# The first pair's queries in two column halves, its keys in one transfer, and an order that allows for late landings

## The chip, the cores and the metric

The kernel runs on one core of a Trainium2 chip. The metric is the device time of one execution in microseconds (us), the median of several runs. One more execution was recorded by the hardware profiler. Its span runs from the first instruction to the last, and all times of day below are counted from the start of that span.

The engines are PE (TensorE, matrix products and transposes), DVE (VectorE), ACT (ScalarE), POOL (GpSimd) and SP (SyncE, which here only issues transfers). Each engine works through its own list of instructions strictly in order: an instruction that waits holds everything behind it on that engine.

## What is computed

Attention with 4 batches and 8 heads of 768 tokens and 64 channels, in which a query sees only the keys of its own hash bucket, and behind it a gated layer over all 3072 tokens:

```
q_bits = (q @ proj > 0);  k_bits = (k @ proj > 0)          # 6 bits for each token
mask   = bucket(q_bits)[:, None] == bucket(k_bits)[None, :]
scores = where(mask, q @ k.T / sqrt(64), -1e9)
attn   = exp(scores - max);  attn = attn / (sum(attn) + 1e-9)
x      = attn @ v                                           # gathered to (3072, 512)
out    = (sigmoid(x @ w_gate) * (x @ w_val)) @ w_out        # 512 -> 1536 -> 512
```

## The kernel before

The kernel works on pairs of heads. There are 16 pairs, and each has six steps of 128 queries, in two groups of three (NG = 2, GT = 3). Pair 0 differs from the others: nothing runs ahead of it, so its preparation stands open at the start of the program.

The names that matter are these. `kr` and `wide` (later `qr`) are the keys and queries as loaded, `vr` the values. `tk`, `tq` and `ts` are their transposes on PE; `ts` is the query block with the two heads swapped. `kx`, `qx` and `sx` are copies of the transposes in SBUF. Each is split into a high part (`kh`, `qh`, `qsh`) and a low remainder (`kl`, `ql`, `qsl`), so that three products give nearly full precision. `hw` holds the projection, and `w0` (row name `w`) a padded copy of it, made on DVE by `hash_weights`. `hk` and `hq` are the hash products of pair 0, and `kb` and `qb` the bits that come out of them. One score task (`sc`) is a product of bits plus three products of high and low parts. `e` is the masked minimum of the scores, then their exponential; `tp` is its transpose, `ef` the copy of that, `pv` the product with the values, `rd` and `rb` the way of the row sums through memory, and `xs` the result, stored to `xd`.

The gated layer's weights come as 64-bit numbers. `converted` loads one (`raw...`) and rebuilds it as 32-bit numbers in four DVE passes, one ACT pass and one POOL pass; `split` makes its high and low parts, and for most of them writes these out to a kept copy in memory (`kg`, `kv`, `ko`), from where `fetch_piece` brings them back when the gated layer proper begins. Ten such pieces form one slot; the first slot's names are `wg_4`, `wv_4` and `wo_4`. The products of the early part of the gated layer (`zg`, `zv`, `zo`) are mixed with the attention of the next batch; the steps `z1g`, `z2g` and so on and `yo` follow after it.

A planner sets the order of everything. Each task has a key (its priority, in steps of attention), an engine or several to choose from, a duration, and the tasks that it follows. `Plan.order` plays this through in time, and the tasks are written out in the order in which it starts them. For a transfer it assumes a time to landing. For PE it also knows three forms of tiles (rows for `sc` and the transposes, columns for `pv` and the later hashes, all for the 128x128 products), and it stays in one form for as long as `PATIENCE` allows. Thirty products without a use (`busy`, row name `idle`, 128x512) fill PE where the plan has nothing else for it. Keys `W_KEY` and `W_STEP` set when a weight may be loaded and how far apart the weights lie.

## Time and profile before

| what | value |
|---|---|
| median of 3 runs | 999.85 us (997.95 to 1000.48) |
| the profiled execution's own time | 997.94 us |
| its span | 996.2 us |
| PE busy | 969.6 us, 97% of the span |
| DVE busy | 775.6 us (78%) |
| ACT busy | 554.0 us (56%) |
| POOL busy | 271.9 us (27%) |
| moved by DMA | 190.95 MB, mean 192 GB/s |

The profiled execution lies 1.74 us above its span and at the lower end of the timed runs. A busy PE need not be useful: the fillers count as busy, and so does a product that runs at half clock.

### The profile page before, as it was taken

To read this page: it belongs to the slowest core of one execution; us is meant where nothing else is said; L and a number is where in the kernel's file an instruction comes from. 1 tells how busy PE (TensorE), PEld (TensorE's weight loads), DVE (VectorE), ACT (ScalarE), POOL (GpSimd) and SP (SyncE) were. 2 spreads that over 40 slices of the span, in tenths; PEclk is the share of its full clock that TensorE was granted. 3 is DMA by queue.
4 is the path that set the end of the run, shared out by engine and by line. 5 is a ranking of instruction groups with operands and counts; after the bars stand their busy time and mean duration, and the time that the engine had idled before them with its cause. 6 is when DMAs were issued, how large, how long until landed. Compare 5 with 4: busy or idle time off the path is not lost.

```text
span 996.2 us, 20856 instructions
## 1 busy us (share of the span) xinstructions
PE 969.6 (97%) x8092; PEld 777.3 (78%) x8092; DVE 775.6 (78%) x1460; ACT 554.0 (56%) x1015; POOL 271.9 (27%) x245
## 2 busy tenths in 40 slices
PE   7999999999999999899999999999999999999998
PEld 4555567676666666666689989989989999999897
DVE  6778888897889778687567879887687778787864
ACT  4868788787877778787643434333323325242330
POOL 2252566546666556552012131100000000000000
PEclk9999999999999999999999999999999999999999
DMA  6456576667776766656368969477479570514121
GB/s 134 125 135 169 162 203 202 209 200 217 233 211 222 236 194 204 190 169 236 107 233 292 356 234 354 171 234 276 141 233 337 198 275 16 175 44 147 43 85 63
DMA packets 144250, 190.95 MB, mean 192 GB/s; under 512 B 64632, under 2 KB 102936, under 8 KB 144152
## 3 DMA queue, kind: packets, MB, share of 16 engines
q1 hardware_dynamic: 142520, 189.24, 59.2%
q8 instruction: 63, 1.03, 0.4%
q10 hardware_dynamic: 1568, 0.39, 0.2%
q14 instruction: 35, 0.29, 0.1%
q0 software_dynamic: 64, 0.00, 0.0%
HBM read 127.41 MB, written 49.28 MB: 177 GB/s over the span
## 4 chain that ended last, share of the span: by engine, by line
PE 83%; DVE 7%; DMA 4%; ACT 3%; SPq 2%; issue 1%; POOL 1%; DVEq 0%; ACTq 0%; POOLq 0%
PE yo L876 17%; PE pv L1235 10%; PE sc L1167 7%; PE tp L1218 6%; PE zv L535 3%; PE zo L568 3%; PE sc L1161 3%; PE zg L535 3%; DVE e L1177 3%; PE z1g L757 2%; PE z7g L757 2%; PE z4v L757 2%; PE z1v L757 2%; PE z5g L757 2%; PE z4g L757 2%; PE z3g L757 2%
## 5 line engine op out<-in xcount | busy, mean ns | idle before, releaser
L1185 ACT ACTIVATE e<-e,st 128x768 f32<-128x768 f32 x192 | 178.7, 932 | 50.0 <-DVE e L1177 49.6
L1177 DVE TENSOR_SCALAR_CACHE_REDUCE e<-sc 128x768 f32<-128x768 f32 x192 | 176.0, 952 | 23.4 <-PE sc L1167 22.4
L1235 PE MATMUL pv<-ef,vr 128*64 128x384 f32 x768 | 139.5, 495 | 0.0
L1218 PEld LDWEIGHTS tp<-ident,e 64*128 64x128 f32 x2304 | 83.8, 138 | 42.2 <-issue 16.6
L1225 DVE COPY ef<-tp 128x768 f32<-128x768 f32 x93 | 87.7, 951 | 20.2 <-PE tp L1218 20.0
L1218 PE MATMUL tp<-ident,e 64*128 64x64 f32 x2304 | 96.3, 226 | 7.0 <-DVE e L1177 3.4
L1225 ACT COPY ef<-tp 128x768 f32<-128x768 f32 x99 | 77.7, 794 | 27.3 <-PE tp L1218 26.9
L1235 PEld LDWEIGHTS pv<-ef,vr 128*64 128x64 f32 x768 | 48.8, 136 | 53.8 <-issue 47.3
L1167 PE MATMUL sc<-kh,ql 64*128 64x384 f32 x192 | 90.2, 470 | 0.0
L1167 PE MATMUL sc<-kh,qsl 64*128 64x384 f32 x192 | 90.1, 469 | 0.0
L1161 PE MATMUL sc<-kb,qb 64*128 64x384 bf16 x384 | 65.0, 331 | 9.5 <-DVE e L1177 5.8
L1167 PE MATMUL sc<-kh,qh 64*128 64x384 f32 x192 | 64.2, 335 | 0.0
L1167 PE MATMUL sc<-kh,qsh 64*128 64x384 f32 x192 | 64.2, 334 | 0.0
L1167 PE MATMUL sc<-kl,qsh 64*128 64x384 f32 x192 | 64.0, 334 | 0.0
L1167 PE MATMUL sc<-kl,qh 64*128 64x384 f32 x192 | 64.0, 333 | 0.0
L1161 PEld LDWEIGHTS <-qb 64*128 64x128 bf16 x384 | 22.2, 94 | 49.3 <-issue 41.1
L777 ACT COPY snm1g<-z1g 128x384 f32<-128x384 f32 x20 | 9.6, 478 | 84.4 <-PE z1g L757 84.3
L1245 POOL TENSOR_TENSOR xs<-xs,rb 128x384 f32<-128x384 f32 x32 | 33.4, 1044 | 69.1 <-DVE xs L1242 41.9
L876 PE MATMUL yo<-wo,gh 128*128 128x512 f32 x144 | 44.5, 390 | 0.0
L1056 POOL TENSOR_TENSOR kl<-kx,kh 128x768 fp32r<-128x768 f32 x16 | 29.3, 1833 | 42.1 <-ACT kh L1053 26.1
L915 DVE TENSOR_TENSOR ol<-yo,ol 128x512 f32<-128x512 f32 x36 | 24.8, 688 | 19.6 <-PE yo L876 19.4
L535 PE MATMUL zg<-xh,wg 128*128 128x384 f32 x128 | 37.5, 348 | 0.1
(591 smaller groups left out, 2812.7 us busy)
## 6 DMA issues: line engine op xcount, KB each, us to landing
wg<-kg SPq DMA_DIRECT2D x33, 512.0 KB
wv<-kv SPq DMA_DIRECT2D x33, 512.0 KB
ra<-xd SPq DMA_DIRECT2D x32, 384.0 KB
wo<-ko SPq DMA_DIRECT2D x22, 512.0 KB
part<-ob SPq DMA_DIRECT2D x36, 256.0 KB
kg<-pkg SPq DMA_DIRECT2D x15, 512.0 KB
kv<-pkv SPq DMA_DIRECT2D x15, 512.0 KB
kr<-in_k_dram SPq DMA_DIRECT2D x64, 96.0 KB
```

What stands on the lines that cost most here:

```text
L535: nc.tensor.matmul(z["acc"][:, :GN], a[:, wc], x[xx][c // 2][:, c % 2, :], start=(c == 0 and i == 0), stop=(c == KC - 1 and i == 2),)
L568: nc.tensor.matmul(acc, a[:, slot, ts_], w, start=(first and i == 0), stop=(last and i == 2))
L757: nc.tensor.matmul(bank[m], a[:, wc], x[xx, block][:, c, :], start=(c == 0 and i == 0), stop=(c == 1 and i == 2),)
L876: nc.tensor.matmul(accs[t], a[:, ts_], w, start=(start and jj == 0 and q == 0), stop=(stop and jj == 1 and q == 2),)
L1161: nc.tensor.matmul(sc[:, j, :GN], z["qb"][rows, beyond if j else c], z["kb"][rows, h], start=True, stop=False, tile_position=(j * D, 0),)
L1167: nc.tensor.matmul(sc[:, j, :GN], q_[rows, c], z["k" + x][rows, h * GN : (h + 1) * GN], start=False, stop=(m == 2), tile_position=(j * D, 0),)
L1177: nc.vector.tensor_scalar(sp(e), gz["sc", t, h][:, :, :GN], MASKED, None, op0=ALU.min, op1=ALU.min, accum_out=gz["st", t][:, h : h + 1],)
L1185: nc.scalar.activation(e, e, AF.Exp, bias=st[:, h : h + 1], scale=-1.0, accum_out=gz["su"][:, h * GT + t : h * GT + t + 1],)
L1218: nc.tensor.transpose(tp[:, r, at_ : at_ + D], gz["e", t, h][rows, c * P : (c + 1) * P], ident[rows, rows], tile_position=(r * D, 0),)
L1225: copy(gz["ef", c].rearrange("p (n r d) -> p r n d", r=2, d=D), gz["tp", c][:, :, :GN].rearrange("p r (n d) -> p r n d", d=D),)
L1235: nc.tensor.matmul(gz["pv"][rows, :GN], z["v"][:, h, c], gz["ef", c][:, h * GN : (h + 1) * GN], start=(c == 0), stop=(c == NC - 1), tile_p ...
L1245: nc.gpsimd.tensor_mul(gz["xs"], gz["xs"], gz["rb"])
```

## The change

Six things change.

1. Keys: each pair's keys come in one transfer (128x2x384) instead of four (128x3x64 each), and `pv` reads the values in the matching order.
2. Projection: its two small transfers are issued by SP, right behind the first keys, instead of by POOL behind its memsets. DVE clears `hw` first of all.
3. Pair 0's queries: `qx`, `qh`, `ql`, `sx`, `qsh`, `qsl`, the query hash and its bits are made in two column halves (`first_pair`). The first group's scores need only the first halves.
4. Planner: transfers may carry a slack (500 to 1500 ns) that is added to the assumed landing before anything that follows is placed.
5. `PATIENCE` goes from 9000 to 12000 for rows and from 1000 to 1500 for columns.
6. Weights: the first load is allowed at key 6 instead of 8, the first six lie 3 apart instead of 2.2, the rest start at key 26 and lie by 2.3.

The core of the diff:

```diff
-PATIENCE = dict(rows=9000, columns=1000, all=1500)
+PATIENCE = dict(rows=12000, columns=1500, all=1500)
...
-                    landed = 0
+                    landed, more = 0, ()
                     if t.dmas:
-                        n_, moved = t.dmas
+                        n_, moved, *more = t.dmas
...
-                    seen = free[e] + (landed or SEEN[e])
+                    seen = free[e] + (landed + sum(more) if landed else SEEN[e])
...
-            nc.gpsimd.dma_start(hw["w"][half * D : (half + 1) * D, at_ : at_ + NB], proj)
+            nc.sync.dma_start(hw["w"][half * D : (half + 1) * D, at_ : at_ + NB], proj)
...
-    W_KEY, W_STEP = 8.0, 2.2
+    W_KEY, W_STEP = 6, 2.3
...
-    def dma(key, nbytes, emit, **kw):
-        return add(key, "sp", 550, emit, dmas=(1, nbytes / 355), **kw)
+    def dma(key, nbytes, emit, slack=0, **kw):
+        return add(key, "sp", 550, emit, dmas=(1, nbytes / 355, slack), **kw)
...
-        a = dma(key, 600000, load, after=after + last_load[late], take=[raw_])
+        a = dma(key, 600000, load, slack=1500, after=after + last_load[late], take=[raw_])
...
-                z[n] = stage1.tile([P, 2, GT, 2, D], F32, name=f"kr{u}", tag="kr", bufs=stock["kr"])
-                from_ = k[b, two].rearrange("h (p c) d -> p h c d", c=NC)
-                for h in range(2):
-                    for j in range(2):
-                        eng.dma_start(z[n][:, h, :, j], from_[:, h, j * GT : (j + 1) * GT])
+                z[n] = stage1.tile([P, 2, NC, D], F32, name=f"kr{u}", tag="kr", bufs=stock["kr"])
+                eng.dma_start(z[n], k[b, two].rearrange("h (p c) d -> p h c d", c=NC))
...
+        def plain_swapped(j, part):
+            if j == 0 and part == 0:
                 z["sx"] = xp.tile([P, S], F32, name="sx", tag="xr1")
-            rows, first = halves[j], (1 - j) * D
-            to = ordered(z["sx"])[rows]
-            from_ = z["t", "s"][rows, :, first : first + GN].rearrange("p r (m d) -> p r m d", d=D)
+            rows, first = halves[j], (1 - j) * D + part * GT * D
+            from_ = z["t", "s"][rows, :, first : first + GT * D].rearrange("p r (m d) -> p r m d", d=D)
+            nc.scalar.activation(ordered(z["sx"])[rows, :, thirds[part]], from_, AF.Copy, scale=-SCALE)
...
+        def plain_half(part, eng):
+            if part == 0:
+                z["qx"] = stage1.tile([P, S], F32, name=f"qx{u}", tag="qx", bufs=1)
+            to, from_ = ordered(z["qx"])[:, :, thirds[part]], turned_("q")[:, :, thirds[part]]
...
+        def high_half(x, part, copy):
+            if part == 0:
+                for a_ in "hl":
+                    z[x + a_] = at.tile([P, S], F32R, name=f"{x}{a_}{u}", tag=f"{x}{a_}")
+            copy(z[x + "h"][:, parts_[part]], z[{"q": "qx", "qs": "sx"}[x]][:, parts_[part]])
...
+        def low_half(x, part, eng):
+            c = parts_[part]
+            eng.tensor_sub(z[x + "l"][:, c], z[{"q": "qx", "qs": "sx"}[x]][:, c], f(z[x + "h"][:, c]))
...
+        def hash_first(n, which):
+            if which[0] == 0:
+                z["hs", n] = ps2.tile([P, 2, 512], F32, name=f"h{n}{u}", tag="two")
+            hs = z["hs", n]
+            for m in which:
...
+        def first_pair(needs):
+            both = dict(take=["port"], give=["port"])
+            swap = add(t0 - 2.95, "pe", 2 * NC * TH, turn_swapped, after=[here["q"], last_turn], take=["two"], kind="turn")
+            kh_ = add(t0 - 3.9, "act", 735, lambda: high("k", nc.scalar.copy), after=plains)
+            kl_ = add(t0 - 3.9, "pool", 1850, lambda: low("k", nc.gpsimd), after=[kh_])
+            hk = add(t0 - 3, "pe", 4 * MM * 2, lambda: hash_first("k", (0, 1)), after=plains + [hw["task"]], take=["two"])
+            kb_ = add(t0 - 3.5, "dve", 560, lambda: bits_first("k", 0), after=[hk])
+            kb2 = add(t0 - 3.49, "dve", 560, lambda: bits_first("k", 1), after=[hk], give=["two"])
+            needs[0].extend([kl_, kb_, kb2])
+            last, hq = None, None
+            for p_ in range(2):
+                n_ = t0 - 2.9 + 2.4 * p_
+                qx = add(n_, [("dve", 480, lambda p_=p_: plain_half(p_, nc.vector)), ("act", 430, lambda p_=p_: plain_half(p_, nc.scalar))][:1 + p_],
+                         after=[last_turn, last], take=["qx"] * (p_ == 0), give=["two"] * p_)
+                last = qx
+                hq = add(n_, "pe", 4 * MM, lambda p_=p_: hash_first("q", (p_,)), after=[qx, hw["task"], hq], take=["two"] * (p_ == 0))
+                qb_ = add(n_ + 0.1, "dve", 560, lambda p_=p_: bits_first("q", p_), after=[hq], give=["two"] * p_)
+                qh = add(n_, [("dve", 300, lambda p_=p_: high_half("q", p_, nc.vector.tensor_copy)), ("act", 430, lambda p_=p_: high_half("q", p_, nc.scalar.copy))][:1 + p_],
+                         after=[qx])
+                ql = add(n_, "dve", 480, lambda p_=p_: low_half("q", p_, nc.vector), after=[qh], **both)
+                sx = add(n_, "act", 430, lambda p_=p_: plain_swapped(0, p_), after=[swap])
+                swap = sx = add(n_, "act", 430, lambda p_=p_: plain_swapped(1, p_), after=[sx], give=["two"] * p_)
+                sh = add(n_, [("act", 430, lambda p_=p_: high_half("qs", p_, nc.scalar.copy)), ("dve", 300, lambda p_=p_: high_half("qs", p_, nc.vector.tensor_copy))],
+                         after=[sx])
+                sl = add(n_ + 0.1, [("dve", 480, lambda p_=p_: low_half("qs", p_, nc.vector)), ("pool", 950, lambda p_=p_: low_half("qs", p_, nc.gpsimd))][:1 + p_], after=[sh], **both)
+                needs[p_].extend([qb_, ql, sl])
+            heads_done.extend(needs[0] + needs[1])
...
+            n: add(t0 - 10.72, "act" if i == 0 and n == "q" else "sp", 1300 if n == "q" else 600,
+                   lambda n=n: load(n, nc.scalar if i == 0 and n == "q" else nc.sync), dmas=(2, 1860, 500 * (i > 0)) if n == "q" else (1, 1360, 500 * (i > 0)), take=[n + "r"],
+                   after=(first_loads[:3] if i == 1 else first_loads if i == 2 else []) + [last_loads.get(n)])
...
-            first_loads.extend(here.values())
-            hw["loaded"] = add(t0 - 10.5, "pool", 1200, load_projection)
-            hw["landed"] = add(0, "timer", 0, lambda: None, after=[hw["loaded"], add(0, "timer", 4000, lambda: None)])
...
+            hw["loaded"] = add(t0 - 10.5, "sp", 1100, load_projection, after=[here["k"]] * 0, dmas=(2, 60))
+            hw["task"] = add(t0 - 10, "dve", 1300, hash_weights, after=[hw["loaded"]])
+            first_loads.extend(list(here.values()) + [hw["loaded"]])
...
+            attend(i, g, z, needs if i else needs[0] + needs[1] * g, v_here)
...
-        key += W_STEP
+        key += 3
+    key = 26
```

Since the planner sees other numbers, the order changes nearly everywhere. Three places show it. First, the head of SP's list, before:

```order
L967 DMA kr_0_241<-in_k_dram 128x3x64 x4
L980 DMA vr_0_262<-in_v_dram 128x2x384
L967 DMA kr_1_277<-in_k_dram 128x3x64 x4
L976 DMA qr_1_325<-in_q_dram 128x6x64 x2
L980 DMA vr_1_335<-in_v_dram 128x2x384
```

and now:

```order
L964 DMA kr_0_239<-in_k_dram 128x2x384
L283 DMA hw<-in_proj_dram 64x6 x2
L977 DMA vr_0_257<-in_v_dram 128x2x384
L964 DMA kr_1_272<-in_k_dram 128x2x384
L973 DMA qr_1_304<-in_q_dram 128x6x64 x2
```

The four transfers of the first keys became one, and the projection's two stand right behind it, ahead of the first values.

Second, DVE's list in the preparation of pair 0, from the last copy of the projection (`w`) to the last low part that the first scores need, before:

```order
L294 COPY w_220<-hw 64x2x12
L1045 TENSOR_SCALAR qx_0_312<-tq_0_282 128x2x6x64
L1053 CAST qh_0_320<-qx_0_312 128x768
L1025 TENSOR_SCALAR kb_172<-hk_0_317,dk_206 128x384
L1025 TENSOR_SCALAR kb_172<-hk_0_317,dk_207 128x384
L1056 TENSOR_TENSOR ql_0_321<-qx_0_312,qh_0_320 128x768
L1022 TENSOR_SCALAR qb_170<-hq_0_329,dq 128x768
L1008 TENSOR_TENSOR qsl_0_338<-sx,qsh_0_337 128x768
```

and now:

```order
L294 COPY w_220<-hw 64x2x12
L1000 TENSOR_SCALAR qx_0_307<-tq_0_274 128x2x3x64
L1008 CAST qh_0_315<-qx_0_307 128x384
L1000 TENSOR_SCALAR qx_0_307<-tq_0_274 128x2x3x64
L1012 TENSOR_TENSOR ql_0_316<-qx_0_307,qh_0_315 128x384 x2
L1030 TENSOR_SCALAR kb_172<-hk_0_312,dk_206 128x384
L1030 TENSOR_SCALAR kb_172<-hk_0_312,dk_207 128x384
L1028 TENSOR_SCALAR qb_170<-hq_0_324,dq 128x384
L1012 TENSOR_TENSOR qsl_0_331<-sx,qsh_0_330 128x384
L1028 TENSOR_SCALAR qb_170<-hq_0_324,dq 128x384
```

Each pass over 768 query columns became two over 384. The second half of `qsl` is gone from DVE (it stands on POOL now), and the bits of the second half stand behind everything that the first group's scores need.

Third, SP's list around the last kept weight of the attention stage (`ko_109`), up to the first fetch of a kept piece (`wg_4`), before:

```order
L1199 DMA rd_94<-sv_2_0_7772 4x32x32
L419 DMA ko_109<-pko_109_7713 128x1024
L1062 DMA qsh_3_7786<-qh_3_7776 64x768 x2
L1206 DMA rb_2_0_7794<-rd_94 64x384 x2
L1062 DMA qsl_3_7837<-ql_3_7777 64x768 x2
L1079 DMA qb_171<-qb_171 24x384 x2
L1086 DMA kb_173<-qb_171 12x384 x4
L980 DMA vr_3_7934<-in_v_dram 128x2x384
L1248 DMA xd_65<-xs_1_1_7903 128x384
L726 DMA wg_4_00_7966<-kg_0_116 128x1024
```

and now:

```order
L1224 DMA rd_97<-sv_3_1_8360 4x32x32
L419 DMA ko_109<-pko_109_8354 128x1024
L1231 DMA rb_3_1_8414<-rd_97 64x384 x2
L1273 DMA xd_65<-xs_3_0_8421 128x384
L726 DMA wg_4_00_8451<-kg_0_116 128x1024
```

The last kept weight stood right behind the store of row sums of the last batch's third pair (`sv_2_0`); now it stands behind that of the last group of all (`sv_3_1`), and the fetches follow after that.

On PE the list now opens with 9 fillers instead of 11, and between `hq` and the first score stand 7 instead of 13.

## Rows read from the trace of the kernel before

**Rows 1.** Windows of core 0: three stages; stretch, its length, busy time by engine, clock, DMA.

```profile
18.20:150.00 131.80, 122.51 (x1551) 79.10 (x1550) 108.33 (x223) 103.81 (x193) 54.98 (x43) 1.00 0.56 152
150.00:490.00 340.00, 332.19 (x3804) 228.55 (x3802) 275.64 (x542) 264.26 (x480) 180.83 (x160) 0.99 0.67 206
490.00:992.20 502.20, 501.85 (x2680) 463.34 (x2674) 380.46 (x655) 180.49 (x337) 30.42 (x28) 1.00 0.56 193
```

**Rows 2.** Timeline, 0 to 18.3: start, length, engine, line, operation [idle before].

```profile
0.75 2.35 SPq L967 DMA_DIRECT2D kr<-in_k_dram  x4
...
3.26 1.20 POOL L283 DMA_DIRECT2D hw<-in_proj_dram  x2
...
6.79 0.40 PE L1033 MATMUL tk<-ident,kr 64*128 64x64 f32 x6 [0.85 <-DMA kr<-in_k_dram]
...
6.99 0.57 PE L1033 MATMUL tq<-ident,wide 64*128 64x64 f32 x12
7.22 0.81 ACT L1049 ACTIVATE kx<-tk 128x768 f32<-128x768 f32 x1 [4.99 <-PE tk L1033]
...
8.65 0.17 DVE L288 TENSOR_SCALAR hw<-hw 64x6 f32<-64x6 f32 x1 [0.41 <-DMA hw<-in_proj_dram]
...
8.98 1.80 POOL L1056 TENSOR_TENSOR kl<-kx,kh 128x768 fp32r<-128x768 f32 x1 [4.52 <-ACT kh L1053]
...
9.13 1.69 DVE L293 COPY w<-hw 64x24 f32<-64x24 f32 x1
...
10.94 0.96 DVE L1045 TENSOR_SCALAR qx<-tq 128x768 f32<-128x768 f32 x1
...
10.97 2.19 PE L1014 MATMUL hk<-kx,w 128*128 128x384 f32 x4 [2.97 <-DVE w L294]
...
13.20 1.14 DVE L1025 TENSOR_SCALAR kb<-hk,dk 128x384 bf16<-128x384 f32 x2 [0.71 <-PE hk L1014]
...
14.26 0.95 DVE L1056 TENSOR_TENSOR ql<-qx,qh 128x768 fp32r<-128x768 f32 x1
...
15.31 2.97 PE L308 MATMUL idle<-sig 128*128 128x512 bf16 x13
...
15.52 1.02 DVE L1022 TENSOR_SCALAR qb<-hq,dq 128x768 bf16<-128x768 f32 x1 [0.31 <-PE hq L1014]
...
18.21 0.34 PE L1161 MATMUL sc<-kb,qb 64*128 64x384 bf16 x2
```

**Rows 3.** Windows with a low granted clock, columns as in Rows 1.

```profile
11.70:15.00 3.30, 3.30 (x7) 1.79 (x6) 2.56 (x5) 0.00 (x0) 0.00 (x0) 0.50 1.25 224
...
412.00:414.00 2.00, 2.00 (x10) 1.56 (x8) 1.41 (x4) 1.55 (x3) 1.49 (x2) 0.50 0.86 301
```

**Rows 4.** Timeline around 407: DVE, then PE.

```profile
407.29 0.43 DVE L364 TENSOR_SCALAR exv<-rawv 128x512 int32<-128x512 int32 x1 [5.36 <-DMA rawv<-in_moe_w_val_dram]
...
409.45 0.34 PE L1161 MATMUL sc<-kb,qb 64*128 64x384 bf16 x2 [2.80 <-DVE e L1177]
```

**Rows 5.** Waits, whole span: engine, line, waited for; us, times, longest.

```profile
DVE exv L364 <- DMA rawv<-in_moe_w_val_dram: 8.5, 5, 5.4
```

**Rows 6.** The chain that ended last, 363 to 376: one and two tasks of `pv`.

```profile
367.23 1.44 PE pv L1235 x8
...
369.93 2.73 PE pv L1235 x16
```

**Rows 7.** Timeline of SP's queue, 425 to 560.

```profile
451.43 0.41 SPq L419 DMA_DIRECT2D ko<-pko  x1
...
461.98 1.98 SPq L726 DMA_DIRECT2D wg<-kg  x4
...
485.62 0.56 SPq L1199 DMA_DIRECT2D rd<-sv  x1
```

**Rows 8.** The chain that ended last, 500 to 520.

```profile
511.94 1.05 PE z1g L757 x6
...
515.09 4.16 PE zv L535 x24
```

More of the change, by code (lines that the diff above doesn't have):

```diff
@@ L238, in lsh_attention_glu_kernel @@
     nc.gpsimd.memset(zero, 0.0)
+    hw = {"w": const.tile([P, HB], F32, name="hw")}
+    nc.vector.memset(hw["w"], 0.0)
     warm = const.tile([P, 1], F32, name="warm")
@@ L418, in split @@
             return low_, low_
-        return low_, dma(key, 1024 * size, lambda: nc.sync.dma_start(to, f(z["w"])), after=[low_], give=[wk])
+        return low_, dma(key, 1024 * size, lambda: nc.sync.dma_start(to, f(z["w"])), slack=1000, after=[low_], give=[wk])
     made_piece = {}
@@ L509, in low @@
             eng.tensor_sub(z["xl"][m][:, k_], z["xr"][m][:, k_], f(z["xh"][m][:, k_]))
-        a = add(FIRST, "sp", 1050, load, after=stored + in_turn["x"], take=["xr"], dmas=(2, 2600))
+        a = add(FIRST, "sp", 1050, load, after=stored + in_turn["x"], take=["xr"], dmas=(2, 2600, 1000))
         z["ready"], prev = [], None
@@ L1000, in plain_swapped @@
                 eng.activation(to, from_, AF.Copy, scale=-SCALE)
-        def high_swapped(copy):
-            for x in "hl":
-                z["qs" + x] = at.tile([P, S], F32R, name=f"qs{x}{u}", tag=f"qs{x}")
-            copy(z["qsh"], z["sx"])
-        def low_swapped(eng):
-            eng.tensor_sub(z["qsl"], z["sx"], f(z["qsh"]))
-        def hash_first(n):
-            z["hs", n] = hs = ps2.tile([P, 2, 512], F32, name=f"h{n}{u}", tag="two")
-            for m in range(2):
+        def high_half(x, part, copy):
[11 more added lines that the diff above has]
+            for m in which:
                 at_ = P + m * P if n == "k" else 0
@@ L1086, in spread_k @@
                     eng.dma_start(z["kb"][j * D + h * HS : j * D + (h + 1) * HS, h], z["qb"][at_ : at_ + HS, :GN])
-        if i == 0:
-            pass
+        def first_pair(needs):
[25 more added lines that the diff above has]
+            heads_done.extend(needs[0] + needs[1])
+            add(0, "sp", 0, lambda: None, after=[ql, hq], give=["qx"])
+            add(0, "sp", 0, lambda: None, after=[kl_, hk], give=["kx"])
@@ L1090, in pair @@
+        needs = [[], []] if i == 0 else []
         here = {
-            n: add(t0 - 10.72, "act" if i == 0 and n == "q" else "sp", 1300 if n == "q" else 2100,
-                   lambda n=n: load(n, nc.scalar if i == 0 and n == "q" else nc.sync), dmas=(2, 1820) if n == "q" else (4, 1760), take=[n + "r"],
-                   after=(first_loads[:2] if i == 1 else first_loads if i == 2 else []) + [last_loads.get(n)])
+            n: add(t0 - 10.72, "act" if i == 0 and n == "q" else "sp", 1300 if n == "q" else 600,
+                   lambda n=n: load(n, nc.scalar if i == 0 and n == "q" else nc.sync), dmas=(2, 1860, 500 * (i > 0)) if n == "q" else (1, 1360, 500 * (i > 0)), take=[n + "r"],
+                   after=(first_loads[:3] if i == 1 else first_loads if i == 2 else []) + [last_loads.get(n)])
@@ L1109, in pair @@
             )
[L1110 to L1124 removed]
+            if i or n == "k":
+                plains.append(add(
+                    n_, [("act", 690, lambda n=n: plain_(n, nc.scalar)), ("dve", 870, lambda n=n: plain_(n, nc.vector))][:1 + (i > 0)],
+                    after=[last_turn], give=["two"], take=[n + "x"],
+                ))
+        if i == 0:
+            first_pair(needs)
         else:
@@ L1139, in pair @@
             needs.append(c_)
-            if n == "q" and i:
-                needs += [add(n_, "sp", 1200, lambda x=x: swapped(x), after=[y], dmas=(2, 1530)) for x, y in (("h", b_), ("l", c_))]
+            if n == "q":
+                needs += [add(n_, "sp", 1200, lambda x=x: swapped(x), after=[y], dmas=(2, 1530, 1000)) for x, y in (("h", b_), ("l", c_))]
         if i == 0:
-            first_loads.extend(needs)
-        v_here = dma(t0 - 5, 490000, load_v, take=["vr"], after=first_loads[:2] + [last_loads.get("v")])
+            first_loads.extend(needs[0])
+        v_here = dma(t0 - 5, 490000, load_v, slack=500, take=["vr"], after=first_loads[:3] + [last_loads.get("v")])
         last_loads["v"] = v_here
         for g in range(NG):
-            attend(i, g, z, needs, v_here)
+            attend(i, g, z, needs if i else needs[0] + needs[1] * g, v_here)
     def attend(i, g, z, needs, v_here):
@@ L1269, in attend @@
         a = add(n, "sp", 680, told, after=[a], dmas=(1, 80), give=["sv"])
-        spread_ = add(n, "sp", 1250, spread, after=[a], dmas=(2, 680), take=["rb"])
+        spread_ = add(n, "sp", 1250, spread, after=[a], dmas=(2, 680, 1000), take=["rb"])
         chunks, last = {}, None
```

44 lines of the change are left out of this document (12 added, 32 removed).

## The prediction

> **What bounds the kernel now.** I read the windows by stage first, since one mean over the span hides that the stages have different limits. Behind 490 us PE is busy for 501.85 of 502.20 us and the chain that ended last is nothing but PE products [rows 1, 8]: no order can gain anything there, only lose. From 18.2 to 490 us PE is busy for 454.7 of 471.8 us, so 17.1 us are waits: 9.3 in the first 131.8 us, where no product of the gated layer can fill in yet, and 7.8 behind that [rows 1]. In front of it stands the preparation of pair 0. The first score starts at 18.21 us, and the 13 fillers ahead of it [rows 2] show that much of PE's busy time there is no work. So there are two places to gain: 18.2 us ahead of the first score, and 17.1 us of waits.
>
> The timeline of the start shows what the first score waits for, back from its end [rows 2]. The fillers run from 15.31 to 18.28 and let it in at 18.21, although its last bits were ready by 16.54 and the last low part behind them (as long as `ql`, 0.95) by about 17.5. The hash products `hk` and `hq` fill 10.97 to 15.31. `hk` waited 2.97 us for `w`, the copy of the projection. That copy waited for the projection itself, whose second half landed at 8.65, and then one of its passes took 1.69 us where its neighbour on DVE took 0.17, because POOL was working on `kl` from 8.98 to 10.78. The projection was issued by POOL only at 3.26, so it landed 4.7 us after its issue. And PE, having stood idle before `hk`, ran at a granted clock of 0.50 from 11.70 to 15.00, the 1.2 GHz level [rows 3].
>
> **The change, part by part.** *The projection.* On SP it stands behind one key transfer. Four of these took 2.35 us to issue [rows 2], one takes 0.59, so the two issues start at about 1.35 and 1.95. How soon they land on this queue no row shows. It could be not sooner than the keys in front of them (6.75, by the wait of `tk` [rows 2]), or almost at once, in which case the keys alone gate `hk`. I take the same 4.7 us as on POOL's queue, because the same loads are on their way: 6.05 and 6.65. From the landing at 8.65 to `hk` at 10.97 passed 2.32 us, of which 1.52 were the long copy's excess; 0.8 remain, so `w` is ready at 7.5 instead of 10.97.
>
> *The keys.* The last of four parts landed at 6.75 [rows 2]. One transfer is wholly issued 1.76 us sooner, but PE can no longer begin with a part. Bounds: 5.0 (the whole 1.76 gained) to 6.75 (none of it); I take the middle, 5.8. Then `tk` ends near 6.25, `kx` (0.81) near 7.1, and POOL's `kl`, which began 0.95 after `kx` ended, runs from about 8.0 to 9.8 (1.80). The queries landed before 6.99, when `tq` began; their issue is not changed, so `tq` and `ts` (together 1.0 us, 6.99 to 8.0) end at about 7.5 if the queries come at 6.5. `hk` starts then: 7.5, against 10.97.
>
> *The clock.* The products 10.97 to 15.31 ran for 0.73 us before the fall, 3.3 at 0.50 and 0.3 behind it [rows 2, 3]: 2.7 us of work at the full clock. PE fell after standing idle from 8.0 to 10.97. Now `ts` and `hk` nearly touch, and I take the full clock: `hk` ends near 8.9 and `hq` near 10.2, its second half held until the second `qx` half at about 8.9. The seven fillers (2.97/13 = 0.23 each) end near 11.8. Wholly at the 1.2 GHz level they would end at 7.5 + 5.4 + 1.6 = 14.5.
>
> *The halves.* With PE out of the way DVE becomes the path. Its list is `qx`, `qh`, `qx`, `ql` twice, `kb` twice, one `qb`, one `qsl`. The first three lie beside `kl`. The two `ql` halves each read two SBUF tiles. The copy's 1.69 us [rows 2] shows that DVE can be held while POOL works, so I let them start when `kl` ends, 9.8. Half a pass costs half a row: `ql` 0.48 twice, `kb` 1.14, `qb` 0.51, `qsl` 0.48, in all 3.1 us. The first score starts at about 13.0. **Term: -5.2.** Bounds: with the projection at once and the keys at 5.0 the same list ends near 12.1 (-6.1); with nothing landing sooner `w` comes at 9.5, and products as slow as before (4.3) and the fillers (1.6) end near 15.4 (-2.8). The second halves are behind the first score and hidden by its group.
>
> A row bears out half of a rule of the Trainium skill here. SBUF — State Buffer, in SBUF: two separate sides, says that DVE with two SBUF inputs and a reading POOL instruction lock each other out for a whole instruction. The row has a one-input copy held; no row here has `ql` beside `kl`. By the rule the start is the one above; if two-input passes were not held, `ql` would begin at 9.2 and the score at 12.4.
>
> *The order behind.* The slack moves what follows a load later in its engine's list. The clearest stall it addresses: at 407 DVE stood 5.36 us on a weight load with `e` behind it, PE lost 2.80 [rows 4], and the clock then fell to 0.50 [rows 3], another 1.0 us in that window. In all, DVE waited for such value loads 8.5 us in 5 cases [rows 5], this one included. The slack of 1.5 us covers less than a third of 5.36, but other passes may now stand ahead. Bounds: -3.8 when this stall goes, +3.8 when one like it appears elsewhere; nearer to the first, since every assumed landing gets later: **-2.5**.
>
> *Forms of tiles.* Counted over both orders from the first score to the first step, PE changes form 221 times now and 213 before, fillers aside: four more visits. One task of `pv` takes 1.44 us, two in one visit 2.73 [rows 6], so a visit costs 0.15 beyond its work. **+0.6**, at most twice that.
>
> *Fillers.* Between the first score and the first step stand 14 instead of 6. One costs 0.23 and a visit's 0.15, so eight cost 3.0 if each is in the way and nothing where PE waits anyway. Most stand in the first three pairs, inside the 9.3 us of waits [rows 1]: **+1.0**.
>
> *Keys' issue in the other 15 pairs:* 15 x 1.76 us less on SP. SP is not on PE's path except through late landings, so I count it with the -2.5. *`hw` cleared first* moves one short memset past another: nothing.
>
> *The late weights.* The last kept piece went out at 451.43, the fetches began at 461.98, and the first step that needs them ran at 511.94 [rows 7, 8]. Now that piece stands behind the last row sums (485.62 [rows 7]; some 6 us sooner now), so fetches begin near 484, and the order puts the first step behind `zv`, whose end was 519.25 [rows 8], so at about 513. The reserve between fetch and step shrinks from 50 us to 29. I price it at nothing; what it costs without that cover is below.
>
> **The sum.** -5.2 - 2.5 + 0.6 + 1.0 = -6.1. Against the profiled execution's own 997.94 that is 991.8; against the median of 999.85 it is 993.7. The profiled one stands at the low end of a spread of 2.5, so I forecast **993.0**.
>
> **The rivals.** *The start gives less.* The queries' share of the transfer engines may shrink beside key packets that are longer now (runs of 6x64 numbers instead of pieces of 64). If they land at 8.0 instead of before 6.99, PE idles from 6.3 on, as it did ahead of the fall in rows 3, `hk` starts at 9.0, and products as slow as before make the list 9.0 + 4.3 + 1.6 = 14.9 at best: the start gives 3.3, and the total is about 995. DMA: Bandwidth & Descriptors, in Queues, rings and completion order, says that each engine takes turns between rows at packet granularity, which speaks for it. For it also stands that the start was already full of transfers; against it that the queries came before 6.99 beside as many bytes. Chance 0.18.
>
> *All stalls behind landings go.* Then the waits fall by some 6 instead of 2.5 and the total is near 989.5. Against: most of the 17.1 us are waits for DVE with no load behind them. Chance 0.10.
>
> *The order gives the start back.* The stall at 407 goes, one like it comes elsewhere, and the fillers are all in the way: -5.2 + 0 + 3.0 + 0.6 = -1.6, which is 997.5; with the old stall kept beside the new one it is 1001. So many rows moved that this cannot be excluded. Chance 0.12.
>
> *Slower: the weights come too late.* If the conversions in front of the last kept piece run late on DVE, ACT and POOL, the fetch does, and PE stands at its first step, with nothing to fill in. This decides from 29 us of delay on, us for us, and 10 us beyond it give 993 + 10 = 1003. For it: the piece moved by three groups of scores. Against: DVE has 64.4 us free between 150 and 490 [rows 1]. Chance 0.07.
>
> **How the numbers follow.** Forecast 0.53, less at the start 0.18, stalls gone 0.10, given back 0.12, late weights 0.07. A measurement of this kernel tells about 0.3% (3 us) from no change. Faster by more takes the first and third in full and most of the second: 0.77; the given-back case and the rest of the second are the same: 0.16; slower 0.07. The range runs from the stalls gone together with a start of -6.1 (988) to a little beyond the order giving back (998.5).
>
> **What would show it.** Right: first score between 12 and 14 us; `hk` starting below 8.2 with no window at 0.50 ahead of the first score; `ql` starting when `kl` ends; waits of PE behind the first score below 17 us; DVE's wait for weight loads clearly below 8.5 us; PE busy without a break from the first step. Wrong: the first score behind 15 us, a DVE or PE wait above 2.5 us in a new place, or PE waiting for `wg` near 510 us.

## The result, and the profile after

| | before | after |
|---|---|---|
| median | 1000.16 us (997.95 to 1003.04, 4 runs) | 986.08 us (983.60 to 986.83, 4 runs) |
| the profiled execution's own time, its span | 997.94, 996.2 us | 986.46, 984.6 us |
| first score | 18.21 us | 14.93 us |
| from the first score to PE's end | 974.0 us | 965.8 us |

The ratio is 0.9853, with a 95% interval of 0.9822 to 0.9884. The kernel became faster, as forecast, but by about twice as much: 986.08 us lies below the range of 988 to 998.5. The profiled spans differ by 11.6 us: 3.3 at the start and 8.2 behind the first score; the rest lies behind PE's end. (The medians differ by 14.1, since the profiled execution of before lies 2.2 us under its own median and that of after 0.4 above.)

The windows of the changed kernel, with the columns of [rows 1]: the three stages, the whole from the first score on, and one microsecond of the preparation.

```profile
14.93:150.00 135.07, 131.15 (x1630) 87.06 (x1630) 114.03 (x233) 111.69 (x202) 51.08 (x38) 1.00 0.54 155
150.00:490.00 340.00, 336.39 (x3847) 229.79 (x3846) 269.11 (x529) 268.93 (x491) 186.83 (x167) 1.00 0.63 199
490.00:980.75 490.75, 489.41 (x2558) 454.07 (x2556) 376.51 (x649) 174.96 (x329) 27.78 (x26) 1.00 0.57 201
14.93:980.75 965.82, 956.95 (x8031) 770.92 (x8030) 759.65 (x1408) 555.58 (x1021) 265.69 (x230) 1.00 0.59 194
...
10.00:11.00 1.00, 1.00 (x2) 0.61 (x3) 1.00 (x3) 0.78 (x2) 0.00 (x0) 0.50 1.07 349
```

Before, the three stages had 9.3, 7.8 and 0.35 us without PE, 17.4 in all [rows 1]; now 3.9, 3.6 and 1.3 us, 8.9 in all. PE's busy time behind the first score is 956.55 before and 956.95 now. So nearly all that was gained there is waiting.

The timeline of the start, columns as in [rows 2]:

```profile
1.25 1.26 SPq L283 DMA_DIRECT2D hw<-in_proj_dram  x2
...
2.55 0.65 SPq L977 DMA_DIRECT2D vr<-in_v_dram  x1
...
3.75 1.29 SPq L973 DMA_DIRECT2D qr<-in_q_dram  x2
...
5.03 0.59 PE L1038 MATMUL tk<-ident,kr 64*128 64x64 f32 x12
...
7.03 0.17 DVE L294 COPY w<-hw 64x24 f32<-64x24 f32 x1
...
7.41 1.82 POOL L1063 TENSOR_TENSOR kl<-kx,kh 128x768 fp32r<-128x768 f32 x1 [4.10 <-ACT kh L1060]
...
8.20 0.91 PE L1038 MATMUL tq<-ident,wide 64*128 64x64 f32 x12 [2.58 <-DMA wide<-in_q_dram]
...
9.78 2.42 PE L1020 MATMUL hk<-kx,w 128*128 128x384 f32 x4
...
10.47 1.22 DVE L1012 TENSOR_TENSOR ql<-qx,qh 128x384 fp32r<-128x384 f32 x2
...
13.78 1.00 POOL L1012 TENSOR_TENSOR qsl<-sx,qsh 128x384 fp32r<-128x384 f32 x1 [4.55 <-ACT qsh L1008]
14.06 1.13 DVE L1012 TENSOR_TENSOR qsl<-sx,qsh 128x384 fp32r<-128x384 f32 x1
...
14.93 0.34 PE L1186 MATMUL sc<-kb,qb 64*128 64x384 bf16 x2
```

The projection is ready at 7.20 (`hk` could begin on it at 10.97 before), and all keys are turned by 5.6 us, against 7.2 [rows 2]. But the queries are there only at 8.20, so PE stands idle for 2.58 us in front of `tq`, and the hash products fall to the 1.2 GHz level (granted clock 0.50).

One loss comes from the change itself: DVE's half of `qsl`, which the first scores need, runs beside the half that went to POOL. It takes 1.13 us, where the same pass alone takes 0.55 (e3), and the first product with `qsl` can start only at 15.24, right behind its end at 15.19.

DVE's waits for weight loads and the two largest sums of PE's waits, between 14 and 490 us, before:

```profile
DVE exv L364 <- DMA rawv<-in_moe_w_val_dram: 8.2, 4, 5.4
DVE exg L364 <- DMA rawg<-in_moe_w_gate_dram: 2.9, 2, 2.4
```

```profile
PE sc L1161 <- DVE e L1177: 5.8, 9, 2.8
PE tp L1218 <- DVE e L1177: 3.4, 7, 1.1
```

and in the changed kernel:

```profile
DVE exv L364 <- DMA rawv<-in_moe_w_val_dram: 0.9, 1, 0.9
DVE exg L364 <- DMA rawg<-in_moe_w_gate_dram: 0.7, 2, 0.4
```

```profile
PE sc L1186 <- DVE e L1202: 3.1, 4, 1.3
PE tp L1243 <- DVE e L1202: 1.1, 1, 1.1
```

In the whole span the value loads alone cost DVE 8.5 us before [rows 5], and the longest PE wait was 2.80 [rows 4]. Now no wait of PE behind the first score is longer than 1.3.

The late weights: SP's queue, and the chain that ended last.

```profile
476.73 0.32 SPq L419 DMA_DIRECT2D ko<-pko  x1
480.92 1.87 SPq L726 DMA_DIRECT2D wg<-kg  x4
```

```profile
505.76 1.04 PE z1g L757 x6
```

The fetch begins 24.8 us ahead of the first step that needs it (50 us before [rows 7, 8]), and PE does not wait for it.

### The profile page after: what moved, and what is told of

Its sections match the earlier page's. It is cut to its first block, busy times and chain, and to the rows that moved or that the text cites. A ratio compares the mean times of both kernels' runs of the same rounds, so it can differ in the third digit from the quotient of the medians.

```text
span 984.6 us, 20831 instructions
## 1 busy us (share of the span) xinstructions
PE 968.0 (98%) x8092; PEld 776.7 (79%) x8092; DVE 768.8 (78%) x1450; ACT 562.2 (57%) x1032; POOL 271.2 (28%) x244
## 4 chain that ended last, share of the span: by engine, by line
PE 87%; DVE 6%; DMA 3%; ACT 2%; SPq 1%; issue 1%; POOL 0%; DVEq 0%; ACTq 0%
PE yo L876 17%; PE pv L1260 11%; PE sc L1192 8%; PE tp L1243 6%; PE zo L568 4%; PE zg L535 3%; PE sc L1186 3%; PE zv L535 3%; PE z1g L757 2%; PE z4v L757 2%; PE z1v L757 2%; PE z3g L757 2%; PE z6g L757 2%; PE z7g L757 2%; PE z5g L757 2%; PE z2g L757 2%
## 5 line engine op out<-in xcount | busy, mean ns | idle before, releaser
L1250 DVE COPY ef<-tp 128x768 f32<-128x768 f32 x90 | 84.4, 949 | 24.7 <-PE tp L1243 24.6
L1250 ACT COPY ef<-tp 128x768 f32<-128x768 f32 x102 | 80.4, 795 | 22.6 <-PE tp L1243 21.9
L915 DVE TENSOR_TENSOR ol<-yo,ol 128x512 f32<-128x512 f32 x36 | 24.8, 689 | 20.8 <-PE yo L876 20.7
L1192 PEld LDWEIGHTS sc<-kh,qsl 64*128 64x128 f32 x192 | 37.3, 194 | 0.7 <-issue 0.6
```

The lines of the kernel that those rows point to most:

```text
L1192: nc.tensor.matmul(sc[:, j, :GN], q_[rows, c], z["k" + x][rows, h * GN : (h + 1) * GN], start=False, stop=(m == 2), tile_position=(j * D, 0),)
L1250: copy(gz["ef", c].rearrange("p (n r d) -> p r n d", r=2, d=D), gz["tp", c][:, :, :GN].rearrange("p r (n d) -> p r n d", d=D),)
```

## The experiments

**How they are compared.** Each was timed beside the kernel before on the same chip; that kernel's medians there were 998.64 (e1 to e4), 998.32 (e5 to e8), 998.15 (e9 to e12), 997.58 (e13 to e16) and 999.66 us (e17, e18). Behind the first score I compare the *length* from there to PE's end and not PE's idle time, because in several profiles a few PE products have no record: the changed kernel profiled a second time shows 8024 products and 2.3 us less busy time than the 8031 above, at a length of 965.74 against 965.82. What the expectations call waits holds up to 2 us of this. A length is that of one execution, though, and this execution lay as much as 4.7 us below its kernel's median (e2, the fastest of its ten) and 3.3 above it (e10). Where lengths and medians disagree, the medians count; between chips they too are sure only to 2 or 3 us, as those of the kernel before show.

### Why the first queries land late

e6, the old form of the key transfers in the changed kernel:

```diff
-z[n] = stage1.tile([P, 2, NC, D], F32, name=f"kr{u}", tag="kr", bufs=stock["kr"])
-eng.dma_start(z[n], k[b, two].rearrange("h (p c) d -> p h c d", c=NC))
+z[n] = stage1.tile([P, 2, GT, 2, D], F32, name=f"kr{u}", tag="kr", bufs=stock["kr"])
+from_ = k[b, two].rearrange("h (p c) d -> p h c d", c=NC)
+for h in range(2):
+    for j in range(2):
+        eng.dma_start(z[n][:, h, :, j], from_[:, h, j * GT : (j + 1) * GT])
...
```

(The planner's entry for these transfers and the order in which `pv` reads the values go back with them.)

> The changed kernel, but every pair's keys again in four transfers of 128x3x64, all else as changed. If the single key transfer is what makes the first queries land late (at 8.2 us instead of before 7.0): the first transpose of queries starts near 7.0 again, that of keys near 6.5 instead of 5.0, and the first score comes at 14 to 15 all the same. If the queries are late for what stands behind the keys on the queue, they land at 8 or later here too. Theory K (fewer issues on SP are what removed the waits behind the first score): the waits rise from 8.9 to 14 or more, 991 to 994. Theory S: they stay below 12.

e7, loads held back in the changed kernel (e18 is the same kernel again, beside the changed one as e17):

```diff
             z["v"] = at.tile([P, 2, NC, D], F32, name=f"vr{u}", tag="vr", bufs=stock["vr"])
+            if i == 0:
+                nc.scalar.copy(z["v"][:, 0, 0, :1], z["kx"][:, :1])
...
-                   after=(first_loads[:3] if i == 1 else first_loads if i == 2 else []) + [last_loads.get(n)])
+                   after=(first_loads[:3] + [hw["values"]] if i == 1 else first_loads if i == 2 else []) + [last_loads.get(n)])
...
-        v_here = dma(t0 - 5, 490000, load_v, slack=500, take=["vr"], after=first_loads[:3] + [last_loads.get("v")])
+        v_here = dma(t0 - 5, 490000, load_v, slack=500, take=["vr"], after=first_loads[:3] + [last_loads.get("v")] + plains[:1] * (i == 0))
+        if i == 0:
+            hw["values"] = v_here
```

> The changed kernel, but the first pair's values and the second pair's keys and queries are issued only behind the first copy of the keys' transposes (about 7 us; ACT writes one number into the value tile first, which the load then overwrites). If the first queries land late because these loads share the transfer engines with them: the first transpose of queries starts between 6 and 7, the hash products at 7.5 to 8.5 at the full clock, the first score at 12.5 to 13.7, that is 1.2 to 2.4 us sooner than in the changed kernel. If the queries are late for a reason of their own (their descriptors, their issue on ACT), they land near 8 and the first score stays at 14.5 to 15. The order behind it is another one, so the total is 982 to 992 by either.

> The changed kernel itself once more, as the measure on this chip for the one that holds the first values back. Queries land at 8 to 8.6 us, first score near 15, waits behind it 8 to 10 us; 984 to 987.

> The kernel that holds back the first pair's values and the second pair's loads, once more beside the changed one on the same chip. Its first score came 2.9 us sooner and its waits behind it were 0.9 longer. If the start is worth its time in the end: 1.5 to 2.9 us faster than the changed kernel here. If the order gives it back: within 1 us of it.

The timeline of e6:

```profile
3.17 1.19 SPq L283 DMA_DIRECT2D hw<-in_proj_dram  x2
4.40 0.59 SPq L980 DMA_DIRECT2D vr<-in_v_dram  x1
...
7.01 0.56 PE L1041 MATMUL tq<-ident,wide 64*128 64x64 f32 x12
8.11 1.56 PE L1023 MATMUL hk<-kx,w 128*128 128x384 f32 x4
...
13.34 0.34 PE L1189 MATMUL sc<-kb,qb 64*128 64x384 bf16 x2 [0.87 <-DVE qb L1031]
```

and that of e7:

```profile
5.78 0.54 PE L1040 MATMUL tq<-ident,wide 64*128 64x64 f32 x12
6.84 1.56 PE L1022 MATMUL hk<-kx,w 128*128 128x384 f32 x4
...
7.74 1.81 POOL L1065 TENSOR_TENSOR kl<-kx,kh 128x768 fp32r<-128x768 f32 x1 [4.43 <-ACT vr L978]
...
7.86 2.11 DVE L1014 TENSOR_TENSOR ql<-qx,qh 128x384 fp32r<-128x384 f32 x1
...
12.07 0.34 PE L1190 MATMUL sc<-kb,qb 64*128 64x384 bf16 x2 [0.87 <-DVE qb L1030]
```

With four key transfers the queries are there by 7.01, as before. That alone would blame the long key transfer. But e7 keeps that transfer and has the queries by 5.78 (e18: 5.96). What both have in common is that the first values and the second pair's loads start later: values at 4.40 in e6, at 7.78 in e7, against 2.55 in the changed kernel. So it is these loads that delay the queries. The first key transfer is at fault in that it leaves SP free to issue them 1.85 us sooner. Which of these loads counts most is not shown: the second pair's queries moved further than the values, from 6.86 before to 3.75. Nor would e6 show it without e7, since the landing varies (last section): e3, with the early loads of the changed kernel, had the queries at 7.38. In both kernels `hk` takes 1.56 us instead of 2.42, at the full clock.

On one chip e17 measured 986.36 us (985.12 to 988.55; ratio 0.9870, 0.9843 to 0.9896) and e18 983.63 us (983.00 to 984.53; 0.9839, 0.9813 to 0.9866). Their first scores stood at 15.34 and 11.74, their lengths were 965.74 and 966.34. So the 3.6 us at the start are worth 2.7 in the end, as the first of the two theories expected. e7's own 983.55 us (982.66 to 984.87; 0.9840, 0.9796 to 0.9884) agrees. e6 measured 986.94 us (985.17 to 989.67; 0.9875, 0.9829 to 0.9922), no better than the changed kernel although its first score came 1.6 us sooner and its length was 966.2 in the profiled execution. That one was the fastest of its four; where the others lost it no profile shows. Its first score had been expected at 14 to 15.

### Which part of the order removed the waits

Three parts make the order: the slack (S), the patience (P) and the weights' places (W). Each is undone by one piece of

```diff
-                    seen = free[e] + (landed + sum(more) if landed else SEEN[e])
+                    seen = free[e] + (landed or SEEN[e])
...
-PATIENCE = dict(rows=12000, columns=1500, all=1500)
+PATIENCE = dict(rows=9000, columns=1000, all=1500)
...
-    W_KEY, W_STEP = 6, 2.3
+    W_KEY, W_STEP = 8.0, 2.2
...
-        key += 3
-    key = 26
+        key += W_STEP
```

e1 undoes all three, e2, e3 and e4 one each, e9, e10 and e16 two each. e5 is the kernel before with the slack added to the same transfers, and nothing else of the change.

> The changed kernel with all three settings of the order taken back: no slack, the old patience, the old places of the weights. Left are the halves, the keys in one transfer and the projection on SP. First score at 14.9 us in every theory, 3.3 below before. Theory S (the slack makes the rest of the gain) and theory W (the places of the weights make it): waits of PE behind the first score back at about 17 us and a time near 995 to 997. Theory K (the single key transfer frees SP, and the rest of the gain comes from that): waits stay near 9 us and the time near 986 to 988. Theory C (any new order draws its waits anew): anything between 986 and 1000.

> The changed kernel without the slack behind landings, all else kept. Theory S: DVE waits for weight loads again, some 8 to 11 us in all, waits of PE behind the first score 14 to 18 us, time 991 to 996. Theories W and K: no change, 985 to 988, DVE's waits for weight loads below 3 us.

> The changed kernel with the weights at their old places (first at key 8, all 2.2 apart), all else kept. Theory W: waits of PE back to 14 to 18 us, time 991 to 996. Theories S and K: 985 to 988 with DVE's waits for weight loads below 3 us.

> The changed kernel with the old patience (9000 and 1000), all else kept. Theories S, W and K: 985 to 988, the waits as they are. Theory C: 984 to 992, since this too reorders everything behind the first pairs.

> The kernel before, with the slack of the change on the same transfers and nothing else of it. Theory S (slack removes PE's waits wherever it is put): the waits of PE behind the first score fall from some 17 us to 9 to 13, DVE's waits for weight loads fall below 3 us, first score unchanged near 18.2: 990 to 995. Theory C (each order draws its waits anew, slack as good as any other edit): waits anywhere between 9 and 20 us, no link between them and DVE's waits for loads; the time between 990 and 1001.

> The changed kernel with the slack kept, but the old patience (9000 and 1000) and the old places of the weights. With everything old the waits of PE behind the first score were 17.1 us; with everything new 8.9; without the slack alone 17.2, without the weights' places alone 15.0, without the patience alone 13.9. Theory A (the three parts are worth fixed amounts): the slack's 8.3 is all there, waits near 9, 985 to 987. Theory B (they need each other: the slack takes DVE's waits for loads away, but PE still waits for DVE where no product of the gated layer stands ready): waits 14 to 17, DVE's waits for loads below 3 us, 990 to 994.

> The changed kernel with the new places of the weights kept, but no slack and the old patience. Theory A: the weights' 6.1 us is all there, waits near 11, 986 to 989. Theory B: without slack DVE waits for loads as before (5 us or more), waits 14 to 18 us, 990 to 999.

> The changed kernel with the new patience kept, but no slack and the old places of the weights. Theory B (the parts need each other): waits of 14 to 19 us, DVE's waits for loads above 4 us, 990 to 997. Theory A (patience is worth its 5 us by itself): waits near 12, 987 to 990.

| kernel | parts in it | DVE's waits for weight loads | PE's waits for `e` | length | median us | ratio to before |
|---|---|---|---|---|---|---|
| before | none, old start | 11.1 | 9.5 | 974.0 | | |
| e5 | S, old start | 1.1 | 7.7 | 972.7 | 995.17 | 0.9951 (0.9925 to 0.9977) |
| e1 | none | 6.4 | 12.9 | 974.0 | 993.37 | 0.9971 (0.9942 to 0.9999) |
| e9 | S | 0 | 12.5 | 973.6 | 994.56 | 0.9969 (0.9955 to 0.9983) |
| e16 | P | 7.6 | 11.6 | 974.7 | 994.17 | 0.9969 (0.9952 to 0.9987) |
| e10 | W | 8.6 | 10.8 | 981.4 | 999.83 | 1.0021 (1.0003 to 1.0040) |
| e3 | S, P | 0 | 7.5 | 970.8 | 992.49 | 0.9943 (0.9925 to 0.9962) |
| e4 | S, W | 1.9 | 5.2 | 968.7 | 990.93 | 0.9933 (0.9912 to 0.9954) |
| e2 | P, W | 7.9 | 8.4 | 974.9 | 1000.68 | 1.0025 (1.0002 to 1.0047) |
| after | S, P, W | 1.6 | 4.2 | 965.8 | 986.08 | 0.9853 (0.9822 to 0.9884) |

(The waits are sums over 14 to 490 us, those for loads of `raw...` alone.) The views behind four of these rows are, of e1, the first of PE's waits and its length,

```profile
PE sc L1186 <- DVE e L1202: 7.8, 13, 1.8
PE tp L1243 <- DVE e L1202: 4.8, 7, 1.5
```

```profile
16.22:990.21 973.99, 956.85 (x8025) 771.67 (x8030) 757.51 (x1404) 558.95 (x1024) 265.33 (x230) 1.00 0.60 192
```

of e5, the waits of DVE for weight loads and the window of its length,

```profile
DVE exg L364 <- DMA rawg<-in_moe_w_gate_dram: 0.8, 1, 0.8
DVE exv L364 <- DMA rawv<-in_moe_w_val_dram: 0.3, 1, 0.3
```

```profile
19.35:992.02 972.67, 955.60 (x8023) 770.75 (x8022) 761.36 (x1409) 554.48 (x1018) 264.17 (x230) 1.00 0.61 193
```

of e9, the first of PE's waits, and its length,

```profile
PE tp L1243 <- DVE e L1202: 7.5, 10, 1.3
PE sc L1186 <- DVE e L1202: 4.4, 11, 0.7
```

```profile
15.80:989.37 973.57, 957.18 (x8023) 772.39 (x8030) 756.36 (x1408) 553.46 (x1020) 265.92 (x230) 1.00 0.59 192
```

and of e10, its length:

```profile
16.10:997.48 981.38, 960.37 (x8024) 773.43 (x8030) 769.60 (x1416) 551.41 (x1014) 265.03 (x230) 1.00 0.59 191
```

Two things are to be seen. First, the slack does what it is for wherever it stands: DVE's waits for weights fall from 11.1 to 1.1 in the old order and from 6.4 to 0 in e9. But PE gains less by that, 1.3 us of length in e5 and 0.4 in e9, because most of its waits for `e` remain (9.5 to 7.7 and 12.9 to 12.5). By the medians e5 is 3.2 us faster than before (its ratio lies 0.25% to 0.75% below 1); its profiled execution was the slowest of its ten, so its length shows too little. e9 gains nothing on e1. Second, no part is worth anything alone in the changed kernel: S -0.4, P +0.7, W +7.4 us of length against e1 (the medians say +1.2, +0.8 and +6.5). All three together are worth -8.2 (-7.3). Without the slack the weights' places cost 7.4 us (e10), and 6.5 by the medians beside P too (e2 against e16; their lengths differ by 0.2 only because the one profiled execution lay 4.7 below its median and the other 3.1 above). With it they gain (e4 against e9: -4.9, by the medians -3.6; after against e3: -5.0 and -6.4). So theory A, fixed amounts, falls, theory S falls too, and theory B stands. W's own theory, that early weights are what the order needs, holds only where there is slack. K falls: e6 keeps its length of 966.2 without the single key transfer. e2 lost more than any theory had expected (1000.68), and e4's 990.93 lies where only theory C had put it.

The traces tell where the parts meet. In the kernels that have both S and W (the changed one, e4, e6 to e8, e11 to e15, e17, e18) PE has run 24 products `zg` of the gated layer by 150 us, and has stood idle for 3.9 to 6.5 us behind the first score by then. Without the slack, and in e5, it has run 12; e9 and e3, with the old places, have 20 and 24. In all of these it has stood idle for 7.4 to 11.6 us. So without the slack the early places bring no product forward. That these products are what fills the waits is not shown: e3 has as many and waits 9.2 us.

### These kinds of edit, or these very numbers

All have the three parts of the changed kernel at other numbers. e8 sets

```diff
-    W_KEY, W_STEP = 6, 2.3
+    W_KEY, W_STEP = 6, 2.4
```

and e11 raises all three:

```diff
-                    seen = free[e] + (landed + sum(more) if landed else SEEN[e])
+                    seen = free[e] + (landed + 1.3 * sum(more) if landed else SEEN[e])
...
-PATIENCE = dict(rows=12000, columns=1500, all=1500)
+PATIENCE = dict(rows=14500, columns=1850, all=1500)
...
-    W_KEY, W_STEP = 6, 2.3
+    W_KEY, W_STEP = 5, 2.25
...
-        key += 3
-    key = 26
+        key += 3.3
+    key = 27
```

e14, e13 and e15 raise the slack, the patience and the weights' places alone, to the same numbers. e12 lowers all three: slack by 0.7, patience 10500 and 1250, key 7, 2.38, 2.7 and 24.

> The changed kernel with one number moved a little: the weights behind the sixth lie 2.4 steps apart instead of 2.3. It has no meaning of its own and measures how far a small edit of the order throws the waits. Theory W (early weights, then a gap, are what the order needs): waits 8 to 11 us, 984 to 988. Theory C (an order draws its waits anew): 9 to 18 us, and the three neighbours that each undid a part of the order (13.9 to 17.2 us of waits) were draws of the same kind: 986 to 995.

> The changed kernel with all three parts, but other numbers: slack times 1.3, patience 14500 and 1850, weights from key 5, the first six 3.3 apart, the rest from 27 by 2.25. If the kind of edit is what counts, the waits are 8 to 12 us and the time 984 to 989. If it was these very numbers that happened to be good, the waits are 13 to 18 us like those of the kernels that lack a part, and the time 989 to 996.

> The changed kernel with all three parts, but other numbers on the other side: slack times 0.7, patience 10500 and 1250, weights from key 7, the first six 2.7 apart, the rest from 24 by 2.38. If the kind of edit counts: waits of 9 to 13 us, 985 to 990, a little worse than with the full slack. If the very numbers count: 13 to 18 us, 989 to 996.

> The changed kernel with the patience alone raised further, 14500 and 1850, as in the kernel whose three parts all went up and that waited 17.9 us. If the patience was what broke that one (too long a stay in a form makes POOL, ACT and DVE's work late), the waits are 14 to 18 us here, 990 to 995. If not, 8 to 12 us and 984 to 988.

> The changed kernel with the slack alone raised, times 1.3. If a larger slack broke the kernel with all three up (work behind loads is placed too late, and DVE meets it in a bunch), the waits are 14 to 18 us, 990 to 995. If not, 8 to 12 us and 984 to 988.

> The changed kernel with the weights' places alone moved: from key 5, the first six 3.3 apart, the rest from 27 by 2.25. If these broke the kernel with all three up (its DVE waited 6.6 us for gate weights), the waits are 14 to 18 us, DVE's waits for loads 5 us or more, 990 to 995. If not, 8 to 12 us and 984 to 988. If none of the three raised alone breaks it, the waits are a matter of the one order that comes out, and not of a part.

| kernel | first score | length | median us | ratio to before |
|---|---|---|---|---|
| e8, weights by 2.4 | 15.38 | 966.4 | 986.98 | 0.9870 (0.9819 to 0.9922) |
| e12, all three down | 15.13 | 964.4 | 985.72 | 0.9885 (0.9868 to 0.9903) |
| e13, patience up | 15.01 | 965.2 | 985.77 | 0.9884 (0.9864 to 0.9904) |
| e14, slack up | 17.07 | 965.7 | 987.57 | 0.9898 (0.9881 to 0.9916) |
| e15, weights up | 14.35 | 966.2 | 988.31 | 0.9917 (0.9894 to 0.9941) |
| e11, all three up | 14.60 | 975.9 | 993.52 | 0.9956 (0.9941 to 0.9971) |

Five other sets of numbers give a length within 1.4 us of the changed kernel's. So it was not the luck of one order, and theory C is right at most as far as e11 goes. That one loses 10 us of length (7.8 by the median against e12 on the same chip), though each of its parts, raised alone, loses little: e15, the worst of them, is 2.5 us slower than e13 on the same chip, and its 988.31 lies just outside the range for a harmless edit. e11 loses most of it between 150 and 490 us, where PE stands idle for 9.7 us instead of 3.6:

```profile
150.00:490.00 340.00, 330.33 (x3786) 225.82 (x3783) 265.69 (x523) 267.06 (x492) 184.47 (x165) 0.99 0.62 191
```

Its DVE waits 6.6 us for gate weights, in spite of the larger slack. That need not be the cause: in e6 DVE waits 6.4 us for weights at a length of 966.2. Nothing told of the loss beforehand.

## Why the prediction was wrong in its size

**The step that failed: "The order behind".** It was put at -2.5 with a lower bound of -3.8; the waits behind the first score fell by 8.5 us (17.4 to 8.9). I had priced the edit by the one stall that the slack addresses most clearly [rows 3 to 5], and looked for the rest of the gain at landings only. e5 shows what that buys: the stall at 407 and its like go, and with the slack alone in the old order PE gains 1.3 us of length, the kernel 3.2 by the medians. So the term was about right for the slack alone, and too small for the three settings together. What fell are PE's waits for `e` (9.5 to 4.2), `ef` and `qb`, of which the rival "all stalls go" had said that no load stands behind them. That was an argument against a gain, and the runs contradict it. That slack, patience and places do this by what they put ahead of `e` on DVE is likely, but not shown. I had given the other two no gain at all, the patience only a cost (+0.6) and the weights' places only a danger. The bounds were those of a single stall and not of the 17.1 us that the windows showed.

**The start** was mis-sized: -5.2 forecast, -3.3 measured (-2.9 in the second profile of the same kernel, e17). The projection (landed 6.46 for 6.65, `w` at 7.2 for 7.5) and the keys (5.03 for 5.8) came as worked out or sooner. The queries came at 8.20 instead of 6.5. I kept them because "their issue is not changed", and overlooked what SP issues next when it is free sooner. From there on it went as the rival "the start gives less" had it: idle PE, `hk` at 9.8, the clock at 0.50, a start worth 3.3. I had named that rival's cause wrongly, though: longer key packets, and e7 has the same first keys (whether those of the second pair's keys add to the delay no run separates). DMA: Bandwidth & Descriptors of the Trainium skill, in Queues, rings and completion order, says that each engine takes turns between rows at packet granularity. e7, where fewer loads share the engines, agrees with it; no run shows the turns themselves. Where the queries are on time DVE is the path, as the step had it, and the sum of 13.0 is near: e6 reaches its first score at 13.34, with `kl` from 9.0, e7 at 12.07 and e18 at 11.74, with `kl` from 7.74 and 7.42 instead of 8.0. The list counted one pass too many, since the first score waits for `qb` (0.87 us in the row of e7) and not for `qsl` behind it.

**The clock and the halves.** The full clock was right only where the queries came sooner (e3, e6, e7, e18). That `ql` is held by `kl` could not be seen in the changed kernel, where `kl` had ended before. e7 shows it: half of `ql` took 2.11 us beside `kl`, 0.55 behind it. The same then held for DVE's half of `qsl` beside POOL's in the changed kernel (1.13 us), which the step had not priced. The rule of the Trainium skill that was weighed, SBUF — State Buffer, in SBUF: two separate sides, has DVE with two SBUF inputs locked out for the whole POOL instruction; these rows agree, and the start was rightly counted from the end of `kl`.

**Forms and fillers** were put at +1.6; all of PE's busy time behind the first score grew by 0.4. **The late weights** were right at nothing, with a reserve of 24.8 us for the 29 forecast.

In sum: -3.3 and -8.5 in place of -5.2 and -2.5, and +0.4 for +1.6: -11.4 where -6.1 stood. The miss of the start hid a part of the larger one. Still open is by which instructions the three parts act on each other, and why e11 fails.

## What to carry to other kernels

Bound a re-ordering by all the waits that the windows show on the busiest engine, not by the clearest single stall: here the slack that removes the stalls gave 1.3 us of length alone (3.2 by the medians), and the whole order 8.2. When an issuing engine is freed, ask which transfers it now starts sooner, and who shares with them. The three tunings of this planner did not add up, so try each with the others in place, and a few neighbouring settings with it. The best start here (e18) was got by holding back loads that nobody needs yet.

## What the runs showed of the hardware

The landing of one and the same transfer moves by almost two microseconds between executions. Fifteen profiles (the changed kernel, e1 to e4, e8 to e17) issue the same first loads up to 4 us at times that agree within 0.03 us. In them `tq`, which waits for the queries, began between 7.38 (e3) and 9.29 us (e14), and the first score followed at 13.35 to 17.07. In e7 and e18, where until then nothing was issued besides the first keys, the queries and the projection, `tq` began at 5.78 and 5.96, clearly outside this spread; e6, at 7.01, lies just outside.

In the changed kernel TensorE's clock fell after PE had stood idle for 2.58 us ahead of `tq`: `hk` took 2.42 us, with a granted clock of 0.50 (the 1.2 GHz level) from 10 to 11 us. In e3, e6 and e7, with gaps of 1.45, 1.14 and none, it took 1.56 at a granted clock of 1.00.

A DVE pass that reads two SBUF tiles did not end beside a POOL subtraction, but 0.41 to 0.42 us after it, whenever it had begun: `ql` took 2.11 us beside `kl` in e7 and 1.70 in e18, and `qsl` 1.13 beside POOL's half in the changed kernel, where such a pass alone took 0.55.
